# Attention and MLP on one core: first key halves on one queue, one load on GpSimd's queue, more late loads under way, and the last tiles stored by token

## The chip, the core and the metric

The kernel runs on one core of one Trainium2 chip. A core has a matrix engine (TensorE, PE in the profile), three engines for elementwise work (VectorE or DVE, ScalarE or ACT, GpSimd or POOL) and a queue engine (SyncE or SP), which here only starts transfers. ACT and POOL can start transfers too. The engines run side by side; each takes its own instructions strictly in the order in which the program issues them, and they wait for each other through semaphores. The metric is the device time of one launch in microseconds (us), the median of several runs.

## The reference

Linear attention with a product feature map, and behind it an MLP over all tokens. Sizes: batch B = 4, heads H = 4, sequence S = 1088, head dimension D = 32, r = 8; the MLP has width 128 and 2048 hidden units.

```python
def phi(x):                                   # 8 x 8 products per token
    a = np.einsum('rd,bhsd->bhsr', S1, x)
    b = np.einsum('rd,bhsd->bhsr', S2, x)
    return np.einsum('bhsi,bhsj->bhsij', a, b).reshape(*x.shape[:-1], r * r)
q_p, k_p = phi(q), phi(k)
kv = np.einsum('bhsf,bhsd->bhfd', k_p, v)
z = np.sum(k_p, axis=2)
num = np.einsum('bhsf,bhfd->bhsd', q_p, kv)
den = np.einsum('bhsf,bhf->bhs', q_p, z)[..., None] + 1e-06
x = (num / den).transpose(0, 2, 1, 3).reshape(B * S, H * D)
h = x @ w_in
g = np.maximum(h, 0.0) + alpha * np.minimum(h, 0.0)
out = g @ w_out
```

## The kernel before

The kernel builds a list of about 770 steps, and a table written out by hand, ORDER (L24 to L70), puts them into one sequence: each word names a step, the engine that runs it (p TensorE, a ACT, d DVE, g POOL, s SP) and the buffer slots that it takes. `arrange` (L98) reads the table, and the loop at L641 issues the steps in that sequence. So the order on every engine and queue is what ORDER says. A number behind p is a count of dummy work: before this step TensorE multiplies ones, so many blocks of 128 columns, in matmuls of up to 512 (`dummy`, L288).

*Attention.* Each batch has a key part (`keys`, L443) and a query part (`queries`, L509). Keys: two loads `ld_k…`, a transpose on DVE (`k…T`, L430), a feature matmul (`k…f`, L464), a transpose back (`k…fT`, L468), the 8 x 8 products on DVE or POOL (`k…p`, L484), the product with V (`kv…`, L504), a copy (`kvc`), a transpose on TensorE (`fin`) and a copy (`kvR`); beside it the sum over keys (`zs`, `z1`, `zS`, `C`). Queries: turn (`q…T`), feature matmul (`q…f`, L420), transpose (`q…fT`, L423), normaliser (`q…t`, `rc`, `b`), products (`q…p`), transposes (`q…PT`, L527), product with kvR (`q…n`, L534) and copies into the MLP's input (`q…x`, L542). Batch 0 is cut finer, so that work starts early: keys in two halves of 18 and 16 rows (`k0.0`, `k0.1`), queries in three pieces, c and d of 8 rows (loads `qa0`, `qa1`) and b of 18 rows (load `qb`). S1 and S2, one kilobyte each, are the two loads `rows` and `rows_1`; every feature matmul needs them, through `rowsT` (L312), `Wk` and `Wf`.

*MLP* (`mlp`, L571). Ten token tiles: 0 and 1 have 256 tokens, 2 to 8 have 512, 9 has the 256 tokens that are left over (64 of each batch). A tile has 16 steps `h` (x by one 128-column block of w_in, L590), 16 ReLUs `r` on ACT or DVE (L596, L598) and 16 steps `o` (ReLU by (1 − alpha) w_out, summed in one PSUM bank, L583; tile 9: L581), and one step `W` that adds x by w_in diag(alpha) w_out, a matrix built once (`winT`, `w_b`, `w_hi`, `w_lo`, `Wmm`, `W`). Twelve ReLU buffers and eight PSUM banks limit how far h runs ahead of o. Tiles 0 to 8 give the output transposed: a DVE transpose of 32 x 32 blocks (`oT`, L604) and four stores of 128-byte rows, 64 KB each for a 512-token tile (`store_main`, L616). Tile 9 has the tokens as the weights of its o matmuls, so that its sums come out by token, in two banks of 128 tokens; two copies (`oT9.0`, `oT9.1`) and two stores follow.

*Loads* (`load`, L196). All come through SP's queue but three on ACT's (k0.0, S1, alpha). A load of more than 64 KB waits on its queue until the third-last such load before it has landed (AHEAD = 3; six for k0, v0 and qa). V loads also wait for a POOL memset (`pads`, L232). Batch 3 reuses the key and query tiles of batch 0.

## Time and profile before

| | |
|---|---|
| runs | 108.78, 108.81, 109.87 us; median 108.81 |
| the profiled execution | 109.35 us; its span, first to last instruction, 107.6 us |
| PE busy | 97.0 us (90%) |
| PEld (weight loads) | 51.8 us |
| DVE / ACT / POOL busy | 82.8 / 65.4 / 47.2 us |
| read / written | 8.79 MB / 2.23 MB |
| the chain that ended last | PE 59%, DMA 28%, DVE 5%, SP's queue 3% of the span |

A profiled execution records every instruction with its start and its length. The page sums them by engine; the view of the chain follows the work that ended last back from step to step; the timeline lists instructions in order of time, merging neighbours of one kind (x3 is three of them); the stretches give the busy time of each engine between two times. An engine that is busy is not always useful (dummies, a slow clock), and an engine that idles costs nothing unless the end waits for it. The profile marks what ended an idle time with an arrow and the last releaser that it could see.

### The profile page before, as it was taken

The numbers are of one execution on the slowest core, as the hardware profiler recorded it, in microseconds if no ns is written. First come the engines' busy times: TensorE is split into PE (matmuls) and PEld (weight loads), VectorE is DVE, ScalarE is ACT, GpSimd is POOL, SyncE is SP. The second block draws the span as 40 slices with busy tenths as digits, with TensorE's granted clock in tenths as the row PEclk, the third lists the DMA queues.
The fourth block names the chain that finished last, engine by engine and source line by source line (L and its number), as shares of the span: only waits on it lengthen the run. The fifth ranks groups of instructions, "written<-read, shape, count | busy, mean of one in ns | idle before, by whom it ended". The sixth has DMA issues, their size and how long they took to land.

```text
span 107.6 us, 3569 instructions
## 1 busy us (share of the span) xinstructions
PE 97.0 (90%) x1476; PEld 51.8 (48%) x1489; DVE 82.8 (77%) x138; ACT 65.4 (61%) x150; POOL 47.2 (44%) x51
## 2 busy tenths in 40 slices
PE   7829979999989949999999999999999999999940
...
PEclk9995579999999999999999999999999999999998
...
GB/s 80 247 227 226 232 195 223 214 211 229 197 175 168 121 169 244 46 6 0 90 39 42 0 6 0 24 75 126 6 0 11 35 0 96 30 57 62 53 154 70
DMA packets 24769, 11.25 MB, mean 105 GB/s; under 512 B 17696, under 2 KB 22320, under 8 KB 24752
## 3 DMA queue, kind: packets, MB, share of 16 engines
...
HBM read 8.79 MB, written 2.23 MB: 102 GB/s over the span
## 4 chain that ended last, share of the span: by engine, by line
PE 59%; DMA 28%; DVE 5%; SPq 3%; issue 1%; DVEq 0%
PE ps L583 23%; PE ps L590 23%; DMA q<-in_q_dram 12%; DMA k<-in_k_dram 10%; PE ps L534 4%; SPq L200 3%; PE ps L504 3%; DMA v<-in_v_dram 3%; DMA w_in_f<-in_moe_w_in_dram 3%; PE ps L581 2%; PE ps L420 1%; DVE Q__71 L527 1%; DVE T__64 L430 1%; DVE T__65 L430 1%; PE ps L384 1%
## 5 line engine op out<-in xcount | busy, mean ns | idle before, releaser
L590 PE MATMUL ps<-x,w_in_bf 128*128 128x512 bf16 (+1 forms) x142 | 40.4, 356 | 0.4 <-issue 0.2
L590 PEld LDWEIGHTS <-w_in_bf 128*128 128x128 bf16 x160 | 15.0, 97 | 15.5 <-issue 3.1
L583 PEld LDWEIGHTS <-w_a_bf 128*128 128x128 bf16 x144 | 13.7, 98 | 12.8 <-issue 1.3
L192 POOL TENSOR_TENSOR P__69<-F__66 128x1152 f32<-128x1152 f32 (+1 forms) x8 | 15.5, 1948 | 8.0 <-DVE F__66 L192 7.7
L527 DVE STREAM_TRANSPOSE Q__71<-P__69 128x1152 f32<-128x1152 f32 (+2 forms) x9 | 10.4, 1167 | 0.1
L596 ACT ACTIVATE rh__87<-ps 128x512 bf16<-128x512 f32 (+1 forms) x11 | 5.9, 541 | 5.1 <-PE ps L590 5.0
L291 PE MATMUL ps<-const-bfloat16-1.0 128*128 128x512 bf16 (+3 forms) x24 | 7.9, 445 | 1.1 <-PEq L658 0.8
L192 POOL TENSOR_TENSOR P__70<-Fk__67 128x1280 f32<-128x1280 f32 (+1 forms) x4 | 8.6, 2161 | 0.0
L430 DVE STREAM_TRANSPOSE T__64<-k 128x1088 f32<-128x1088 f32 (+2 forms) x5 | 5.4, 1072 | 3.5 <-DMA k<-in_k_dram 3.5
L423 DVE STREAM_TRANSPOSE F__66<-ps 128x1152 f32<-128x1152 f32 (+2 forms) x6 | 5.9, 983 | 2.6 <-PE ps L420 2.0
L534 PE MATMUL ps<-Q__71,kvR 32*32 32x288 f32 (+2 forms) x384 | 7.7, 332 | 0.1
L596 ACT ACTIVATE rh__79<-ps 128x512 bf16<-128x512 f32 (+1 forms) x11 | 5.9, 540 | 1.8 <-PE ps L590 1.6
L596 ACT ACTIVATE rh__84<-ps 128x512 bf16<-128x512 f32 (+1 forms) x10 | 5.6, 558 | 1.0 <-PE ps L590 1.0
L598 DVE TENSOR_SCALAR rh__86<-ps 128x512 bf16<-128x512 f32 (+1 forms) x6 | 3.6, 594 | 3.1 <-PE ps L590 3.0
L185 ACT CAST x<-ps 128x576 bf16<-128x576 f32 (+2 forms) x6 | 3.1, 514 | 4.7 <-PE ps L534 4.6
L596 ACT ACTIVATE rh__85<-ps 128x512 bf16<-128x512 f32 (+1 forms) x8 | 4.3, 541 | 2.6 <-PE ps L590 1.7
L596 ACT ACTIVATE rh__83<-ps 128x512 bf16<-128x512 f32 (+1 forms) x9 | 4.7, 527 | 1.8 <-PE ps L583 1.0
L534 PEld LDWEIGHTS ps<-Q__71,kvR 32*32 32x32 f32 x384 | 4.5, 103 | 2.8 <-DVE F__66 L423 1.1
L596 ACT ACTIVATE rh__86<-ps 128x512 bf16<-128x512 f32 (+1 forms) x9 | 4.7, 526 | 1.2 <-PE ps L590 1.2
L192 POOL TENSOR_TENSOR P__69<-Fk__68 128x1024 f32<-128x1024 f32 (+1 forms) x2 | 4.3, 2166 | 1.7 <-DVE Q__71 L527 1.7
L583 PE MATMUL ps<-rh__86,w_a_bf 128*128 128x512 bf16 (+1 forms) x14 | 4.9, 349 | 0.1
L598 DVE TENSOR_SCALAR rh__81<-ps 128x512 bf16<-128x512 f32 (+1 forms) x7 | 4.1, 593 | 0.8 <-PE ps L590 0.8
...
## 6 DMA issues: line engine op xcount, KB each, us to landing
...
w_in_f<-in_moe_w_in_dram SPq DMA_DIRECT2D x4, 256.0 KB, 3.8
w_out_f<-in_moe_w_out_dram SPq DMA_DIRECT2D x4, 256.0 KB, 4.1
...
k<-in_k_dram ACTq DMA_DIRECT2D x1, 288.0 KB, 2.8
```

What stands on the lines that cost most here:

```text
L192: (nc.vector if e == "dve" else nc.gpsimd).tensor_tensor(out=dst, in0=a, in1=b, op=what)
L200: i = (nc.sync if e == "sp" else nc.scalar).dma_start(dst, src)
L291: nc.tensor.matmul(PS[:, 7, :128 * m], ones(128), ones(128 * m), start=True, stop=True, skip_group_check=True)
L423: return op({"dve": V(4 * n) + 60}, lambda e: nc.vector.transpose(bview(sb(F), [[n, 4], [1, n]]), ps(bf)[:, :, :n]), [o1], [bf, F], name=f ...
L430: os.append(op({"dve": V(n * 32) + 10}, lambda e, lo=lo, n=n: nc.vector.transpose(sb(bT)[:, lo * 32:(lo + n) * 32], src[:, lo:lo + n].rear ...
L504: nc.tensor.matmul(ps(bk)[32 * h:32 * h + 32, :R], v_sb[b][:, h, j], bview(sb(P), [[1, R]], (4 * j + h) * R), start=j == 0, stop=j == JG - ...
L527: ts.append(op({"dve": V(R * n1) + 20}, lambda e, lo=lo, n1=n1: nc.vector.transpose(bview(sb(Q), [[1, R * n1]], lo * R), bview(sb(P), [[1, ...
L534: nc.tensor.matmul(ps(bn)[32 * h:32 * h + 32, g, :n], kvR[b][32 * g:32 * g + 32, y, 32 * h:32 * h + 32], bview(sb(Q)[32 * g:32 * g + 32], ...
L583: nc.tensor.matmul(ps(bo)[:, :n], w, rhs, start=first, stop=end, skip_group_check=True)
L590: nc.tensor.matmul(ps(b)[:, lo:lo + m], w_in_bf[:, c], x(), start=True, stop=True, skip_group_check=len(parts) > 1)
L596: nc.scalar.activation(sb(br)[:, :n], ps(b)[:, :n], ACTF.Relu)
L598: nc.vector.tensor_scalar_max(sb(br)[:, :n], ps(b)[:, :n], 0.0)
```

## The change

1. Both halves of batch 0's keys load through ACT's queue, first and second there; before, the second half was second on SP's.
2. S1 loads through POOL's queue, behind `pads9` and ahead of `ident` (POOL's first step before); ACT's queue loses it. The copy `identb` moves from ACT to POOL.
3. On SP's queue qb stands ahead of V and of all weights, then come all four parts of w_in, then w_out1, w_out2, k1, w_out0, q1, w_out3, and v1 ahead of k3 and of batch 2's V. Loads of v2, v3, q3 may have six under way, k2, q2, k3 and v1 four.
4. ORDER is written anew throughout, with 103 dummy blocks in place of 91.
5. Tile 8 is computed like tile 9: each o step is four matmuls of 128 columns with the tokens as weights, summed in one bank; two copies of 256 columns on ACT take the place of the DVE transpose, and the four stores have rows of 512 bytes.
6. Tile 9's sums run half by half: the o step of each block is split into `o9.c` (first 128 tokens) and `o9.ch` (last 128), each half has its own copy; the first half goes out in one store, the second in two of 64 tokens.

```diff
 ORDER = """
-ld_rows_1:s ident:g ld_k0.0:a ld_rows:a rowsT:p26:0 selP:g zero:d M2:d ld_k0.1:s ld_w_in1:s ld_alpha:a k0T0:d:0 pads:g wz:g table:a Wk:d k0f0:p6:1
-k0T1:d k0f1:p ld_qa0:s M4:d ld_v0_3:s pads9:g identb:a qaT0:d ld_qa1:s k0fT0:d:0 zs00:p5:3 S2m:p:4 k0fT1:d ld_v0:s win1:a ld_v0_1:s qaT1:d S2q:d
-k0F1:a:1 k0p3:d:0 k0p4:d ld_v0_2:s k0p2:d zs01:p z10:a:0 zS0:p8 k0p0:g Wf:a C0:a k0p1:g alT:p:0 alTc:a qcf:p6:2 qcfT:d:0 qct:d:0 qcrc:d:0 qcb:d
-qcp0:d:1 kv00:p:6 kv01:p kv02:p kv03:p ld_w_in0:s win0:a qdf:p:1 qdfT:d:0 kv04:p ld_w_in2:s kvc0:a:0 qdt:g:0 ld_w_out0:s winT0:p:5 ld_qb:s w_b0:g
-qcPT0:d:0 ld_w_out1:s fin0:p3 kvR0:a qcn:p17:1 win2:a ld_k1_1:s winTc0:a qcx0:a oma:d qdrc:d:0 qdb:g qbT:d w_a1:a qdp0:d:0 qdPT0:d:0 qbf:p11:0 qbfT:d:0
...
-h9.7:p:1 r9.1:a:7 h9.14:p:6 r9.9:d:4 o9.4:p o9.15:p st5.3:s r9.8:d:10 st8.3:s o9.0:p st7.3:a o9.3:p r9.7:d:3 st7.0:a o9.8:p o9.9:p o9.2:p o9.7:p o9.1:p
-o9.5:p r9.14:d:2 o9.14:p oT9.1:d oT9.0:a st9.1:s st9.0:a
+ld_k0.0:a pads9:g ld_k0.1:a ld_rows:g ld_rows_1:s zero:d ident:g rowsT:p27:0 ld_qa0:s M2:d k0T0:d:0 ld_qb:s M4:d ld_alpha:a table:a pads:g Wk:d k0T1:d
+wz:g identb:g k0f0:p8:1 k0f1:p4 selP:g Wf:a ld_qa1:s qaT0:d ld_v0_1:s k0fT0:d:0 ld_v0_3:s zs00:p9:0 S2m:p:3 ld_v0:s k0fT1:d zs01:p k0F1:a:1 S2q:d
+ld_v0_2:s z10:a:0 zS0:p8 C0:a qcf:p8:2 k0p4:d:0 k0p2:d k0p3:d ld_w_in0:s win0:a k0p0:g kv00:p:0 ld_w_in1:s alT:p:6 k0p1:g kv01:p kv02:p kv03:p kv04:p
+kvc0:a:0 alTc:a ld_w_in2:s qcfT:d:0 qaT1:d qct:d:0 qcrc:d:0 qcb:d qcp0:d:0 win1:a qdf:p:1 qdfT:d:0 qcPT0:d:0 fin0:p14 kvR0:a qdt:g:0 qdrc:d:0
+ld_w_in3:s ld_w_out1:s qcn:p17:0 qbT:d oma:d qbf:p8:4 win2:a qdb:g qcx0:a win3:a h0.6:p:0 r0.6:a:0 qdp0:d:0 qdPT0:d:0 qbfT:d:0 w_b1:g h0.1:p:1 r0.1:d:1
+h0.14:p:2 r0.14:a:2 qbt:d:0 ld_w_out2:s w_a2:g ld_k1_1:s ld_k1:s ld_w_out0:s ld_q1:s h0.10:p:3 h0.7:p:0 r0.7:d:3 qbrc:d:0 qbb:g r0.10:a:4 h0.3:p:2
+r0.3:a:5 winT1:p:3 h0.11:p:2 qdn:p:4 qdx0:d w_a1:a o0.6:p:0 winTc1:a h0.9:p:1 h0.12:p:4 r0.12:a:0 h0.5:p:5 r0.11:d:6 qbp0:g:0 ld_w_out3:s h1.2:p:6
+r0.5:a:7 r0.9:a:8 h1.6:p:2 w_a0:g k1T0:d:0 winT0:p:3 ld_q1_1:s r1.6:a:9 h1.11:p:4 r1.11:a:10 r1.2:d:11 qbPT0:d:0 o0.11:p h0.4:p:5 h1.7:p:7 o0.10:p
+qbp1:g r1.7:a:4 h1.3:p:1 winTc0:a o1.6:p:2 w_b0:g o0.7:p r0.4:d:3 h1.14:p:4 k1f0:p:6 r1.3:a:9 o1.2:p o1.7:p k1fT0:d:0 o0.5:p h1.9:p:3 r1.9:d:7 o0.3:p
+h0.0:p:1 r0.0:d:5 k1p1:g:1 r1.14:a:4 qbPT1:d ld_k2_1:s o0.1:p h0.2:p:5 r0.2:a:1 h1.1:p:4 o0.9:p h1.5:p:6 r1.5:a:8 h1.12:p:7 r1.12:a:11 o0.4:p zs10:p:3
+r1.1:a:3 ld_k2:s ld_v1:s z11:d:0 h1.10:p:1 r1.10:d:6 o1.11:p ld_v1_3:s w_a3:a o1.5:p ld_v1_2:s o1.9:p o0.0:p q1T0:d:0 o0.2:p qbn:p:4 qbx0:d o1.10:p
+qbx1:a w_hi0:a k1p0:g o1.12:p o0.12:p ld_v1_1:s zS1:p C1:d h0.15:p:1 r0.15:a:0 o1.1:p h2.4:p:3 r2.4:a:3 ld_q2_1:s k2T0:d:1 q1f:p:4 q1fT:d:0 h2.6:p:1
+r2.6:a:11 o1.14:p h2.15:p:3 r2.15:a:4 o0.14:p o0.15:p w_hi1:a w_b2:g h2.1:p:1 r2.1:a:0 o1.3:p h2.13:p:3 h1.15:p:4 r1.15:d:9 r2.13:a:2 q1t:g:0 ld_k3:s
...
+r2.12:a:11 w_b3:g w_lo0:g r2.7:a:4 r2.9:a:1 kv10:p:6 h1.0:p:4 r1.0:a:5 h2.5:p:7 r2.8:d:7 ld_v2_3:s o2.1:p zs20:p:5 kvc1:a:0 h1.13:p:4 o2.4:p r2.5:a:0
+w_hi2:a q1b:d q1p0:d:0 o2.9:p h2.0:p:3 ld_v3_3:s r1.13:d:8 h2.3:p:7 z12:d:0 q1PT0:d:0 r2.0:a:1 h2.10:p:4 o2.12:p zS2:p o2.8:p fin1:p kvR1:d Wmm0:p:3
...
+h9.12:p:3 r9.12:d:11 r8.12:a:1 o8.5:p o8.15:p r9.9:a:8 o8.12:p W8:p r9.7:d:4 o8.7:p h9.8:p:0 h9.6:p:3 r9.8:a:5 W9:p h9.13:p:1 r9.13:a:1 h9.11:p:7
+o8.4:p o9.15:p o9.15h:p h9.4:p:0 h9.1:p:2 st7.1:s o9.10h:p r9.6:d:7 r9.4:d:0 o9.13:p o9.8:p o9.6:p st1.1:s o9.13h:p h9.0:p:1 r9.0:d:1 h9.14:p:3 W9h:p
+o9.6h:p h9.5:p:0 r9.5:d:7 o9.7:p o9.8h:p oT8.0:a:1 st8.1:s o9.2:p o9.9:p r9.1:a:3 o9.4:p r9.11:a:9 o9.11:p o9.11h:p r9.14:a:10 o9.0:p oT8.1:a o9.1:p
+o9.12:p o9.3:p o9.12h:p o9.0h:p o9.14:p st8.0:s o9.5:p oT9.0:a o9.4h:p o9.2h:p st8.3:s o9.5h:p o9.7h:p o9.14h:p o9.3h:p st8.2:s o9.1h:p st9.0:a o9.9h:p
+oT9.1:d st9.1:s st9.2:a
 """
...
@@ -194,10 +195,10 @@
     loads, issued = {}, []
 
     def load(name, eng, dst, src, nbytes, rate, deps=()):
-        ahead = 6 if name[:2] in ("k0", "v0", "qa") else AHEAD
+        ahead = 6 if name[:2] in ("k0", "v0", "qa", "v2", "v3", "q3") else 4 if name[:2] in ("k2", "q2", "k3", "v1") else AHEAD
 
         def emit(e):
-            i = (nc.sync if e == "sp" else nc.scalar).dma_start(dst, src)
+            i = {"sp": nc.sync, "act": nc.scalar, "pool": nc.gpsimd}[e].dma_start(dst, src)
             if nbytes > 65536:
                 if len(issued) >= ahead:
                     tc.add_manual_dep(i.ins, issued[-ahead].name, mybir.DependencyInfo(mybir.DependencyClass.Sync, mybir.DependencyReason.DATA))
@@ -253,10 +254,10 @@
                  dram(v, (b * H * S + JG * g) * D, [[NJ * D, 32], [S * D, H], [1, n * D]]), 32 * H * n * D * 4, 290., deps)
 
     for i, x in enumerate((S1, S2)):
-        load("rows", (("act", "sp")[i],), rows[i:2 * r:2], dram(x, 0, [[D, r], [1, D]]), 1024, 100.)
+        load("rows", (("pool", "sp")[i],), rows[i:2 * r:2], dram(x, 0, [[D, r], [1, D]]), 1024, 100.)
     load("alpha", ("act",), al, dram(moe_alpha, 0, [[128, NC], [1, 128]]), 8192, 200.)
     for i, (lo, n) in enumerate(((0, 18), (18, 16))):
-        load_rows(f"k0.{i}", k_sb[0][:, lo:lo + n], k, 0, lo, n, eng=("act", "sp")[i])
+        load_rows(f"k0.{i}", k_sb[0][:, lo:lo + n], k, 0, lo, n, eng="act")
     for i in range(2):
         load_rows(f"qa{i}", q_sb[0][:, 8 * i:8 * i + 8], q, 0, 8 * i, 8)
     load_v(0, [c_pads])
@@ -568,20 +569,22 @@
         src, os = turned(f"q{b}", q_sb[b], [got(f"q{b}")])
         xs[b] = queries(b, f"q{b}", src, os[0], JG)
 
-    def mlp(g, parts, store, final=False):
+    def mlp(g, parts, store, final=0):
         n = sum(m for m, _, _ in parts)
-        bo = Buf("ps", 2 if final else 1)
-        seq, done = [], [0]
-
-        def acc(rhs, w):
-            first, end = done[0] == 0, done[0] == NC
-            done[0] += 1
-            if final:
+        bo = Buf("ps", 2 if final == 2 else 1)
+        seq, done = [], [0, 0]
+
+        def acc(rhs, w, half=None):
+            first, end = done[half or 0] == 0, done[half or 0] == NC
+            done[half or 0] += 1
+            if final == 2:
+                nc.tensor.matmul(ps(bo)[:, half, :DM], rhs[:, 128 * half:128 * half + 128], w, start=first, stop=end, skip_group_check=True)
+            elif final:
                 for j in range(n // 128):
-                    nc.tensor.matmul(ps(bo)[:, j, :DM], rhs[:, 128 * j:128 * j + 128], w, start=first, stop=end, skip_group_check=True)
+                    nc.tensor.matmul(ps(bo)[:, 128 * j:128 * j + 128], rhs[:, 128 * j:128 * j + 128], w, start=first and j == 0, stop=end, skip_group_check=True)
             else:
                 nc.tensor.matmul(ps(bo)[:, :n], w, rhs, start=first, stop=end, skip_group_check=True)
-        cost = {"pe": 56 * n / 128 if final else n / 2.4 + 2.6}
+        cost = {"pe": 56 if final == 2 else 56 * n / 128 if final else n / 2.4 + 2.6}
         for c in range(NC):
             b, br = Buf("ps"), Buf("rh")
             need, lo = [], 0
@@ -597,8 +600,21 @@
                 else:
                     nc.vector.tensor_scalar_max(sb(br)[:, :n], ps(b)[:, :n], 0.0)
             seq.append((c, op(AD(n), re, need, [b, br], name=f"r{g}.{c}"), br))
-        last = [op(cost, lambda e, c=c, br=br: acc(sb(br)[:, :n], w_a_bf[:, c]), [o, c_wa[c // 4]], [bo, br], name=f"o{g}.{c}") for c, o, br in seq]
-        last.append(op(cost, lambda e: acc(whole[g](), W_bf), [c_W] + [d for _, _, ds in parts for d in ds], [bo], name=f"W{g}"))
+        halves = []
+        for half in range(2) if final == 2 else (None,):
+            at = bo if half is None else (bo, half, half + 1)
+            last = [op(cost, lambda e, c=c, br=br, half=half: acc(sb(br)[:, :n], w_a_bf[:, c], half), [o, c_wa[c // 4]], [at, br],
+                       name=f"o{g}.{c}" + ("", "h")[half or 0]) for c, o, br in seq]
+            last.append(op(cost, lambda e, half=half: acc(whole[g](), W_bf, half), [c_W] + [d for _, _, ds in parts for d in ds], [at],
+                           name=f"W{g}" + ("", "h")[half or 0]))
+            halves.append(last)
+        if final == 1:
+            boT = Buf("oT")
+            for j in range(2):
+                to = lambda j=j: bview(sb(boT), [[1, 256]], 256 * j)
+                o = op(AD(256), lambda e, j=j, to=to: copy(e, to(), ps(bo)[:, 256 * j:256 * j + 256]), last, [bo, boT], name=f"oT{g}.{j}")
+                store(g, o, boT, to, j)
+            return
         if not final:
             boT = Buf("oT")
             o = op({"dve": V(n) + 60}, lambda e: nc.vector.transpose(sb(boT).rearrange("p j f -> p (j f)")[:, :n], ps(bo)[:, :n]), last,
@@ -607,11 +623,11 @@
             return
         for j in range(2):
             t = consts.tile([128, DM], F32, tag=f"of{j}", name=f"of{j}")
-            o = op(AD(128), lambda e, j=j, t=t: copy(e, t, ps(bo)[:, j, :DM]), last, [(bo, j, j + 1)], name=f"oT{g}.{j}")
+            o = op(AD(128), lambda e, j=j, t=t: copy(e, t, ps(bo)[:, j, :DM]), halves[j], [(bo, j, j + 1)], name=f"oT{g}.{j}")
             store(g, o, t, j)
 
-    def put_out(g, i, o, boT, dst, src):
-        op({"sp": 450, "act": 450}, lambda e: (nc.scalar if e == "act" else nc.sync).dma_start(dst, src()), [o], [boT], name=f"st{g}.{i}", nbytes=65536, rate=150.)
+    def put_out(g, i, o, boT, dst, src, rate=200.):
+        op({"sp": 450, "act": 450}, lambda e: (nc.scalar if e == "act" else nc.sync).dma_start(dst, src()), [o], [boT], name=f"st{g}.{i}", nbytes=65536, rate=rate)
 
     def store_main(b, lo, n):
         def st(g, o, boT):
@@ -620,11 +636,21 @@
                                               ap=[[NJ * DM, 32], [DM, n // 32], [1, 32]]), lambda i=i: sb(boT)[32 * i:32 * i + 32, :n // 32])
         return st
 
+    def store_token_major(b, lo):
+        def st(g, o, boT, src, j):
+            for y in range(2):
+                dst = bass.AP(tensor=out.tensor, offset=(b * S + lo // 32 + 8 * j + 4 * y) * DM, ap=[[DM, 4], [NJ * DM, 32], [1, DM]])
+                put_out(g, 2 * j + y, o, boT, dst, lambda y=y: src()[:, 128 * y:128 * y + 128], 300.)
+        return st
+
     def store_last(g, o, t, j):
-        def f(e):
-            (nc.scalar if e == "act" else nc.sync).dma_start(
-                bass.AP(tensor=out.tensor, offset=(32 + j) * DM, ap=[[NJ * DM, 32], [S * DM, B], [1, DM]]), t)
-        op({"act": 600, "sp": 600}, f, [o], name=f"st{g}.{j}", nbytes=65536, rate=250.)
+        for y in range(1 + j):
+            n = 128 // (1 + j)
+
+            def f(e, y=y, n=n):
+                (nc.scalar if e == "act" else nc.sync).dma_start(
+                    bass.AP(tensor=out.tensor, offset=(32 + j + n // B * y * NJ) * DM, ap=[[NJ * DM, n // B], [S * DM, B], [1, DM]]), t[n * y:n * y + n])
+            op({"act": 600, "sp": 600}, f, [o], name=f"st{g}.{j + y}", nbytes=512 * n, rate=250.)
 
     def cols(b, lo, n):
         return lambda: x_sb[:, b, lo:lo + n]
@@ -635,8 +661,11 @@
     last = len(tiles_)
     whole[last] = lambda: xr.rearrange("p y s b -> p (y s b)")
     for g, (b, lo, n, needs) in enumerate(tiles_):
-        mlp(g, [(n, whole[g], needs)], store_main(b, lo, n))
-    mlp(last, [(256, whole[last], xrs)], store_last, True)
+        if g == last - 1:
+            mlp(g, [(n, whole[g], needs)], store_token_major(b, lo), 1)
+        else:
+            mlp(g, [(n, whole[g], needs)], store_main(b, lo, n))
+    mlp(last, [(256, whole[last], xrs)], store_last, 2)
 
     for o in arrange(ops, classes):
         early[0] &= o.name[:2] != "zs"
```

64 lines of the change are left out of this document (26 added, 38 removed).

## The prediction

> **What bounds the kernel now.** I read three views: the 40 slices for the shape, the chain of work that ended last in order of time, and then the stretches and the timeline where these two disagree with "TensorE is busy".
>
> ```profile
> PE   7829979999989949999999999999999999999940
> PEclk9995579999999999999999999999999999999998
> 2.00:4.00 2.00, 1.71 (x5) 0.44 (x3) 0.44 (x1) 1.16 (x1) 1.34 (x7) 1.00 0.74 190
> 4.00:6.00 2.00, 1.17 (x26) 0.50 (x26) 0.53 (x2) 0.51 (x3) 0.00 (x0) 1.00 0.96 317
> 6.00:8.00 2.00, 0.76 (x17) 0.33 (x18) 1.75 (x5) 0.62 (x1) 0.00 (x0) 0.93 0.71 211
> 8.00:10.00 2.00, 1.98 (x22) 1.12 (x22) 1.57 (x5) 0.61 (x3) 1.95 (x2) 0.50 0.75 198
> 10.00:12.00 2.00, 2.00 (x47) 0.82 (x47) 0.93 (x3) 0.85 (x3) 0.14 (x1) 0.50 0.74 249
> 12.00:14.00 2.00, 2.00 (x93) 1.83 (x96) 1.46 (x6) 0.00 (x0) 0.00 (x0) 0.50 0.76 237
> 38.00:40.00 2.00, 0.50 (x23) 0.35 (x26) 1.62 (x3) 1.99 (x7) 2.00 (x2) 1.00 0.56 142
> ```
>
> Columns of the stretches: length, busy time of PE, weight loads, DVE, ACT, POOL, then granted clock, DMA share, GB/s. From 20 us to 100 us TensorE is full with two exceptions, so what is not TensorE's own work is ahead of 20 us, at 38 to 40 us (1.5 of 2 us idle) and behind the last matmul. From about 8 to 14 us it is busy at half the clock. The 40 slices hide that: they print 9 there.
>
> ```profile
> 4.19 0.27 PE L312 MATMUL ps<-ident,rows 16*32 16x16 f32 x8 [0.48 <-DMA rows<-in_S_dram]
> 4.82 0.53 PE L464 MATMUL ps<-T__64,Wk 64*32 64x144 f32 x16
> 6.01 0.71 DVE L430 STREAM_TRANSPOSE T__64<-k 128x512 f32<-128x512 f32 x1 [1.29 <-DMA k<-in_k_dram]
> 6.87 0.53 PE L464 MATMUL ps<-T__64,Wk 64*32 64x144 f32 x16 [1.51 <-DVE T__64 L430]
> 9.33 1.61 DVE L192 TENSOR_TENSOR P__69<-ps,Fk__67 128x512 f32<-128x512 f32 x3
> 11.97 1.95 PE L504 MATMUL ps<-P__69,v 128*32 128x64 f32 x64
> 14.78 0.37 ACT L185 COPY kvs__76<-ps 128x256 f32<-128x256 f32 x1 [3.21 <-PE ps L504]
> 15.35 0.62 PE L374 MATMUL ps<-identb,w_in_bf 128*128 128x128 bf16 x8 [0.64 <-ACT kvs__76 L185]
> 17.21 0.85 PE L534 MATMUL ps<-Q__71,kvR 32*32 32x64 f32 x64
> 18.15 0.37 ACT L185 CAST x<-ps 128x256 bf16<-128x256 f32 x1
> 19.19 0.50 PE L590 MATMUL ps<-x,w_in_bf 128*128 128x256 bf16 x3
> 22.44 0.71 PE L464 MATMUL ps<-T__64,Wk 64*32 64x288 f32 x16
> ```
>
> Columns: start, length, engine, line, operands, in brackets the idle time before and its releaser. This is the way to the first MLP matmul at 19.19: S1 and S2 land (4.19), the second half of the keys lands (6.0), TensorE has stood still 1.5 us by then, runs at half clock soon after, and reaches kv0 only at 11.97, though its products were ready at 10.94 and its last V quarter, by the queue below, at 9.5. kv0 (its copy waits 3.21 us for it, to 14.78), the query product (17.21) and its copy (18.15) follow one another.
>
> ```profile
> 1.18 1.24 ACTq L200 DMA_DIRECT2D rows<-in_S_dram  x1
> 9.52 0.39 SPq L200 DMA_DIRECT2D w_out_f<-in_moe_w_out_dram  x1
> 18.55 2.22 SPq L200 DMA_DIRECT2D q<-in_q_dram  x2
> 21.07 0.38 SPq L200 DMA_DIRECT2D w_out_f<-in_moe_w_out_dram  x1
> 25.18 0.33 SPq L200 DMA_DIRECT2D v<-in_v_dram  x1
> 27.31 0.33 SPq L200 DMA_DIRECT2D k<-in_k_dram  x1
> 39.61 0.35 SPq L200 DMA_DIRECT2D q<-in_q_dram  x1
> 34.62 1.24 DVE T__64 L430
> 39.68 1.21 PE ps L504 x72
> k<-in_k_dram ACTq DMA_DIRECT2D x1, 288.0 KB, 2.8
> k<-in_k_dram SPq DMA_DIRECT2D x1, 256.0 KB, 4.4
> q<-in_q_dram SPq DMA_DIRECT2D x1, 288.0 KB, 4.8
> ```
>
> An issue on the SP queue waits until the third-last large load before it has landed (L202), so issues date landings: at 9.52 the last V quarter of batch 0 was in, at 21.07 w_in3, at 25.18 w_out3, at 27.31 the second half of k2, at 39.61 the V quarter that kv1 lacked. The last three rows give KB and us from issue to landing. kv1 starts at 39.68: the idle stretch at 38 to 40 us ends on that load as much as on the VectorE step named for it. Adding sizes in issue order, 3.79 MB were in by about 20.4 (second issue of the pair at 18.55), 4.06 MB by 21.07, 4.87 MB by 25.18.
>
> The sum is made against the profiled execution: 109.35 us, span 107.6. It is 0.5 us above the median of 108.81, which the result is taken from.
>
> **The change part by part.** *Head.* k0.1 moves from SP's second place (4.4 us to landing at 6.0) to ACT's second place (1.18, where S1 is now), beside only S2 and qa0 until k0.0 is in; qb must wait for k0.0. Bounds for its landing: 6.0 as now, and 4.0, if it took k0.0's 2.8 us from there. I take 4.85, since 688 KB (both halves and qa0) have to pass, and the stretches moved 0.42 MB by 4.0 (21 and 190 GB/s) and then 317 GB/s. ACT loses the S1 issue (1.24 us) and gains k0.1's; alpha and the table load come no later. The copy identb goes from ACT to POOL, and S1 with it: POOL now issues S1 ahead of ident, M2 and the memsets that SP's V loads wait for. No row shows a POOL DMA. Nearest: the same kilobyte on ACT, 1.24 us to issue and 3.0 us from issue to use; farthest, the slowest load of the three, 4.8 us. Issued at about 1.0, that is use at 4.0 or 5.8. I take 4.2, as now, the nearest row; 5.8 costs 1.1 us of the walk below.
>
> The walk: first turn done at 4.35 and Wk at 4.8; second turn 4.85 to 5.55; second feature product 5.6 to 6.1, ahead of it 4 dummy blocks where the 1.5 us idle was. Dummies are 103 blocks of 128 columns in place of 91, and stand in each of the waits from there to fin0. I take full clock from here. Then transposes to 6.9, S2q at 7.7, products 1.61 us to 9.35, last V quarter 9.6 (1.67 MB instead of 1.64 MB ahead of its end), kv0 9.6 to 10.8 (72 matmuls, 1.21 as at 39.68), copy to 11.4 behind win0, fin0 12.2, kvR0 12.65, 17 dummies, product 13.2 to 14.05, copy to 14.45, qbf, first h at 15.1. Against 19.19 that is −4.1: 1.1 from the earlier keys, 3.0 from the clock. Half of the busy time at half clock (8 to 14, 5.98) gives the same 3.0.
>
> *What the loads take back.* w_in0 to w_in3 now all come ahead of any w_out, and qb ahead of V. k1 ends at 3.80 MB, w_out0 at 4.06, q1 at 4.88: by the landings above 20.4, 21.1 and 25.2, no earlier than their like now. TensorE's written order puts 22 MLP matmuls of 256 columns (2.4 us), winT0, winT1 (0.62 each), qdn (0.85, as at 17.21) and k1f0 (0.71) between first h and o1.2, 5.2 us from 15.1; but k1f0 waits for k1's turn (1.24, as at 34.62) to about 21.8 and ends at 22.5. The order of before has k1f0 ending at 23.15 with 15 MLP matmuls (1.64 us), one winT and qdn done. So it is 0.65 earlier with 1.4 us more done: of the 4.1 us, 2.0 is left there, +2.1. From there to q1f (q1 in at 25.2, plus the turn) TensorE has 4.6 us of written work for 4.0 us, so the 2.0 holds.
>
> *More late loads.* k2, q2, k3, v1 may have four under way, v2, v3, q3 six. By themselves they hide behind TensorE's work; but v1 is moved ahead of q2, k3 and v2 and ends at 6.0 MB, some 31 us, while kv1 comes in the written order at about 31.5. So kv1's idle 1.5 us goes: −1.5. What is late next: DVE has k2's turn ahead of q1fT, k2 lands at about 27.3, as q1f ends; POOL's k1 and q1 products; ACT, which gets nearly all ReLUs there. New stalls between 0 and 1.5 (the one that goes); I take 0.4, nearer to the lower, because the slices show no other of that size from 20 to 100 us.
>
> *Tile 8.* Its 17 output steps become 68 of 128 columns with the tokens as weights.
>
> ```profile
> 93.89 1.29 PE ps L583 x6
> 102.24 1.24 PE ps L581 x22
> 103.50 0.29 DVE of L187
> 103.74 0.67 ACTq L625 DMA_DIRECT2D out_dram<-of  x1
> 104.34 0.60 SPq L625 DMA_DIRECT2D out_dram<-of  x1
> out_dram<-oT__90 ACTq DMA_DIRECT2D x1, 32.0 KB, 1.5
> SPq L669 <- DMA out_dram<-of: 1.5, 1, 1.5
> ```
>
> 68 at 1.24/22 is 3.83 us, 17 at 1.29/6 is 3.66: +0.17. The transpose (DVE, 0.7) becomes two copies on ACT, which has room there. Four stores of 64 KB stay four issues, of 512-byte rows instead of 128-byte.
>
> *End.* The last sums run half by half: the same 34 matmuls, but the first half ends 8 matmuls (0.45 us) before the second, and its copy and store with it. Now: last matmul 103.47, copy to 103.79, SP's last issue at 104.34 behind another store, wait 1.5, end. After: the second half goes out in two stores of 32 KB (1.5 us to landing now) from both queues. ACT's is behind st9.0's issue (0.67), SP's behind st8.2, whose copy stands late in ACT's order. Best: SP free, −1.0; worst: four store issues in line, +0.2. I take −0.4.
>
> Sum: −4.1 + 2.1 − 1.5 + 0.4 + 0.17 − 0.4 = −3.3. 108.8 − 3.3 = 105.5 us.
>
> By the Trainium skill, "DMA: Bandwidth & Descriptors", Specifications, the first byte on the GpSimd path comes after about 1 us, on the sync and scalar path after about 0.6; an estimate by that page puts S1 0.4 us later, and the sum stays at −3.3, since the loads take 2.1 back anyway. No run here shows it.
>
> **The rivals.** *Half clock stays.* The 4.0 to 8.0 stretches show 1.9 us of TensorE work in 4, with no idle longer than 1.5, and the clock fell. The new order fills them with dummies, but much of what is left is 32-column work, and kv0 ran at half clock while busy. Then the head is 1.1 earlier instead of 4.1, nothing is taken back: −1.1 − 1.5 + 0.4 + 0.17 − 0.4 = −2.4, 106.4 us. The Trainium skill, "TensorE: Matmul & The Clock Gate", Part 1, says the clock falls after an idle window of about 3.4 us and that gaps below that are harmless. The trace does not agree: 1.51 us idle was enough, at 0.50 from 8.00. By that rule the idle that this change removes is not the cause and this rival would be the forecast, at 106.4 us.
>
> *The loads take nearly all.* If the weights set the pace to 25 us (ACT's win1 stands ahead of kvR0, win2 ahead of qcx0, each waiting for its load; w_a3 for w_out3) and k2's turn stops DVE, 3.6 is taken back and 1.5 of stalls come again: −4.1 + 3.6 − 1.5 + 1.5 + 0.17 − 0.4 = −0.7, 108.1 us. For it: the MB by time are no better than now. Against: 12 ReLU buffers let h run ahead of o.
>
> *S1 is late; slower.* Place: rowsT, behind it on TensorE everything. If POOL's DMA needs longer than any load shown, TensorE idles from the end of its 27 dummies (3.7), and with the idle comes the half clock (3.0). The terms behind the head give −1.5 + 0.4 + 0.17 − 0.4 = −1.3 with no lead, so it decides once delay plus 3.0 exceeds 5.4, that is S1 in use after 6.6. At 8.0: 3.8 + 3.0 − 4.1 = +2.7, sum +1.4, 110.2 us. For it: no row of a POOL DMA, and ident, M2 and the first turn stand behind its issue. Against: 1 KB.
>
> **How the numbers follow.** One per cent, 1.1 us, is about what a measurement of this kernel can tell from no change; faster is below 107.7. Forecast 0.55 (own range 103.4 to 107.0), half clock 0.17, loads take all 0.17, late S1 0.11. Faster: 0.53 + 0.14 + 0.04 = 0.71; same 0.17; slower 0.12. The range: low is no new stalls (−0.4), the best end (−0.6) and 1.1 less taken back, 103.4; high is 108.6, past the second rival; outside lie late S1 and small ends of the others.
>
> **What would show it.** Granted clock 1.0 from 4 us on; keys' second turn before 5.5; first h near 15; then TensorE gaps before k1f0, up to 22.5; kv1 with no wait near 32; q1n near 40 instead of 44.5; last matmul near 100.2; from it to the end 3.7 instead of 4.1. It would be wrong with S1 in use after 6.6, with k0.1 no earlier on ACT, or with DVE idle for k2 and k3 at 25 to 35.

## The result, and the profile after

The changed kernel takes 114.63 us (median of 4; 114.35 to 115.06), the kernel before 108.8 us beside it: a ratio of 1.0526, 95% interval 1.044 to 1.0612. The forecast was 105.5. The profiled execution took 114.72 us, its span is 112.6 (107.6 before). Medians below are over all executions; the ratios leave out the executions that ran slow throughout, so that the two can differ a little.

Rows picked from the timeline of the changed kernel: TensorE and VectorE up to the first MLP matmul, then TensorE at the end.

```profile
4.56 0.30 PE L313 MATMUL ps<-ident,rows 16*32 16x16 f32 x8 [0.74 <-DMA rows<-in_S_dram]
4.80 1.03 PE L292 MATMUL ps<-const-bfloat16-1.0 128*128 128x512 bf16 x2
5.20 0.71 DVE L431 STREAM_TRANSPOSE T__64<-k 128x512 f32<-128x512 f32 x1
9.63 0.61 PE L292 MATMUL ps<-const-bfloat16-1.0 128*128 128x512 bf16 x2
9.70 1.61 DVE L193 TENSOR_TENSOR P__69<-ps,Fk__67 128x256 f32<-128x256 f32 x3
11.83 0.99 PE L505 MATMUL ps<-P__69,v 128*32 128x64 f32 x56
12.75 0.39 PE L421 MATMUL ps<-qTa,Wf 32*32 32x64 f32 x30
15.49 0.27 PE L421 MATMUL ps<-qTa,Wf 32*32 32x64 f32 x2 [2.35 <-issue]
15.69 1.58 PE L292 MATMUL ps<-const-bfloat16-1.0 128*128 128x512 bf16 x4
17.49 1.95 PE L292 MATMUL ps<-const-bfloat16-1.0 128*128 128x512 bf16 x5
19.37 0.85 PE L535 MATMUL ps<-Q__71,kvR 32*32 32x64 f32 x64
21.18 1.30 PE L593 MATMUL ps<-x,w_in_bf 128*128 128x256 bf16 x6
...
105.86 0.22 PE L581 MATMUL ps<-w_a_bf,rh__85 128*128 128x128 bf16 x1
```

S1 is in use at 4.56 and the keys' second turn is done at 5.91. But two dummy matmuls of 512 columns take 1.03 us at 4.80 and 0.61 at 9.63: TensorE runs at about half speed at 4.80, although the stretches below print a clock of 1.00. kv0 ends at 12.82 (14.71 before), so the head is then 1.9 us ahead. Then TensorE stands still for 2.35 us in the middle of qdf, after 30 of its 32 matmuls, with "issue" as releaser: the profile shows nothing that it waited for. Behind the stop the dummies ahead of fin0 and qcn take 1.58 and 1.95 us, at half clock, and the first h comes at 21.18 instead of 19.19.

The stretches of the same execution (length, busy PE, weight loads, DVE, ACT, POOL; then granted clock, DMA share, GB/s):

```profile
0.00:13.20 13.20, 11.59 (x220) 4.88 (x221) 6.73 (x19) 3.29 (x9) 5.74 (x21) 1.00 0.66 189
13.20:15.40 2.20, 0.00 (x0) 0.00 (x0) 0.69 (x1) 0.65 (x3) 0.00 (x0) 1.00 0.72 207
16.00:18.00 2.00, 2.00 (x8) 1.11 (x7) 1.97 (x7) 0.27 (x1) 1.06 (x3) 0.50 0.96 242
38.00:40.00 2.00, 2.00 (x80) 1.30 (x69) 1.81 (x4) 1.73 (x5) 1.45 (x1) 1.00 0.60 143
```

The clock is at 0.50 from 16 us. The wait of kv1 at 38 to 40 us is gone, as forecast. The stores on SP's queue at the end, and its waits:

```profile
101.49 0.51 SPq L630 DMA_DIRECT2D out_dram<-oT__92  x1
102.06 0.48 SPq L630 DMA_DIRECT2D out_dram<-oT__89  x1
102.58 2.14 SPq L630 DMA_DIRECT2D out_dram<-oT__92  x1
104.76 0.49 SPq L630 DMA_DIRECT2D out_dram<-oT__89  x1
105.29 0.51 SPq L630 DMA_DIRECT2D out_dram<-oT__91  x1
106.33 2.50 SPq L630 DMA_DIRECT2D out_dram<-oT__90  x4
108.92 0.58 SPq L651 DMA_DIRECT2D out_dram<-of  x1
...
SPq L698 <- DMA out_dram<-of: 1.9, 1, 1.9
```

The last matmul ends at 106.08, and SP then has four stores of tile 8 and the last one still to issue. From there to the end it is 6.5 us, 4.13 before. The 5.0 us of span are 2.0 at the first h, 0.6 from there to the last matmul, 2.4 behind it.

### The profile page after: what moved, and what is told of

It reads as the page before. It is cut to its first block, busy times and chain, and to the rows that moved or that the text cites. A ratio compares the mean times of both kernels' runs of the same rounds, so it can differ in the third digit from the quotient of the medians.

```text
span 112.6 us, 3673 instructions
## 1 busy us (share of the span) xinstructions
PE 101.1 (90%) x1541; PEld 53.7 (48%) x1541; DVE 82.9 (74%) x141; ACT 66.1 (59%) x146; POOL 46.9 (42%) x51
## 3 DMA queue, kind: packets, MB, share of 16 engines
q10 hardware_dynamic: 4256, 1.12, 4.5%
## 4 chain that ended last, share of the span: by engine, by line
PE 82%; issue 5%; DMA 3%; ACT 2%; DVE 2%; POOL 0%; DVEq 0%; POOLq 0%; ACTq 0%
PE ps L593 28%; PE ps L586 22%; PE ps L292 7%; PE ps L535 5%; PE ps L505 4%; PE ps L584 3%; PE ps L421 3%; PE ps L465 3%; DMA rows<-in_S_dram 3%; PE ps L581 2%; PE ps L496 1%; DVE T__65 L431 1%; PE ps L375 1%; PE ps L398 1%; PE ps L408 1%
## 5 line engine op out<-in xcount | busy, mean ns | idle before, releaser
L593 PE MATMUL ps<-x,w_in_bf 128*128 128x512 bf16 (+1 forms) x144 | 41.0, 356 | 0.5 <-DVE x L188 0.2
L586 PEld LDWEIGHTS <-w_a_bf 128*128 128x128 bf16 x128 | 12.2, 98 | 11.6 <-issue 2.0
L193 POOL TENSOR_TENSOR P__69<-F__66 128x1152 f32<-128x1152 f32 (+1 forms) x7 | 14.5, 2079 | 1.0 <-DVE F__66 L193 0.8
L528 DVE STREAM_TRANSPOSE Q__71<-P__69 128x1152 f32<-128x1152 f32 (+2 forms) x10 | 11.3, 1126 | 1.4 <-PE ps L535 1.2
L292 PE MATMUL ps<-const-bfloat16-1.0 128*128 128x512 bf16 (+3 forms) x28 | 11.2, 534 | 0.8 <-PEq L687 0.8
L193 POOL TENSOR_TENSOR F__66<-F__66,rd__74 128x288 f32<-128x288 f32 (+2 forms) x4 | 2.1, 532 | 18.8 <-DVE rd__74 L520 12.1
L193 POOL TENSOR_TENSOR P__69<-Fk__67 128x512 f32<-128x512 f32 (+2 forms) x4 | 6.8, 1722 | 3.6 <-DVE Fk__67 L469 3.6
L599 ACT ACTIVATE rh__80<-ps 128x512 bf16<-128x512 f32 (+1 forms) x13 | 7.1, 547 | 1.2 <-PE ps L593 1.1
L599 ACT ACTIVATE rh__78<-ps 128x512 bf16<-128x512 f32 (+1 forms) x11 | 6.1, 559 | 2.2 <-PE ps L593 2.1
L599 ACT ACTIVATE rh__79<-ps 128x512 bf16<-128x512 f32 (+1 forms) x8 | 4.4, 544 | 5.0 <-PE ps L593 5.0
L599 ACT ACTIVATE rh__86<-ps 128x512 bf16<-128x512 f32 (+1 forms) x12 | 6.6, 551 | 1.1 <-PE ps L593 0.6
L599 ACT ACTIVATE rh__84<-ps 128x512 bf16<-128x512 f32 (+1 forms) x10 | 5.8, 575 | 2.0 <-PE ps L593 1.9
L599 ACT ACTIVATE rh__82<-ps 128x512 bf16<-128x512 f32 (+1 forms) x9 | 4.7, 525 | 2.9 <-PE ps L593 2.7
L188 DVE CAST x<-ps 128x576 bf16<-128x576 f32 (+2 forms) x6 | 3.7, 648 | 2.6 <-PE ps L535 2.6
L599 ACT ACTIVATE rh__81<-ps 128x512 bf16<-128x512 f32 (+1 forms) x9 | 4.7, 528 | 0.9 <-PE ps L593 0.9
L292 PEld LDWEIGHTS <-const-bfloat16-1.0 128*128 128x128 bf16 x28 | 2.9, 125 | 4.9 <-issue 4.6
L599 ACT ACTIVATE rh__88<-ps 128x512 bf16<-128x512 f32 (+1 forms) x7 | 3.9, 564 | 2.1 <-PE ps L593 2.1
```

What stands on the lines that cost most here:

```text
L188: nc.vector.tensor_copy(dst, src)
L193: (nc.vector if e == "dve" else nc.gpsimd).tensor_tensor(out=dst, in0=a, in1=b, op=what)
L292: nc.tensor.matmul(PS[:, 7, :128 * m], ones(128), ones(128 * m), start=True, stop=True, skip_group_check=True)
L528: ts.append(op({"dve": V(R * n1) + 20}, lambda e, lo=lo, n1=n1: nc.vector.transpose(bview(sb(Q), [[1, R * n1]], lo * R), bview(sb(P), [[1, ...
L586: nc.tensor.matmul(ps(bo)[:, :n], w, rhs, start=first, stop=end, skip_group_check=True)
L593: nc.tensor.matmul(ps(b)[:, lo:lo + m], w_in_bf[:, c], x(), start=True, stop=True, skip_group_check=len(parts) > 1)
```

## The experiments

Every kernel was timed against the kernel before on the same chip. First h, last matmul and tail (last matmul to end) are read from the timelines.

| run | median us | ratio to before (95%) | first h | last matmul | tail |
|---|---|---|---|---|---|
| before | 108.8 | 1 | 19.19 | 103.47 | 4.13 |
| changed | 114.63 | 1.0526 (1.044 to 1.0612) | 21.18 | 106.08 | 6.52 |
| e1_fill_40 | 112.31 | 1.0309 (1.0243 to 1.0375) | 17.92 | 103.09 | 6.41 |
| e2_store_order | 112.27 | 1.0277 (1.0194 to 1.036) | 20.47 | 105.35 | 5.05 |
| e3_keys_alone | 108.61 | none given | 18.40 | 101.57 | 4.23 |
| e4_ahead_alone | 108.24 | 0.9996 (0.9954 to 1.0037) | 19.30 | 102.05 | 4.45 |
| e5_last_forms | 110.61 | 1.0195 (1.0151 to 1.024) | 18.98 | 103.22 | 5.58 |
| e6_warm_before | 109.34 | 1.0014 (0.9958 to 1.007) | 19.73 | 102.48 | 4.22 |
| e7_qdf_behind | 116.3 | 1.0521 (1.0429 to 1.0614) | 17.11 | 108.33 | 6.57 |
| e8_count | 114.6 | one execution | 20.34 | 106.22 | 6.18 |
| e9_fill_and_end | 111.03 | 1.0223 (1.0177 to 1.0268) | 19.15 | 104.15 | 4.65 |
| e10_tile8 | 110.26 | 1.0129 (1.0077 to 1.018) | 18.48 | 102.37 | 5.43 |
| e11_halves | 109.16 | 1.0002 (0.9966 to 1.0037) | 18.31 | 102.38 | 4.22 |
| e12_new_head | 111.42 | 1.0136 (1.0068 to 1.0204) | 19.60 | 104.62 | 4.18 |
| e13_head_mended | 112.72 | 1.0354 (1.0284 to 1.0424) | 18.12 | 107.01 | 4.49 |
| e14_three_undone | 110.97 | 1.0207 (1.0133 to 1.0281) | 19.58 | 105.62 | 4.48 |
| e15_keys_ahead | 108.18 | 0.9968 (0.9928 to 1.0007) | 19.61 | 102.33 | 4.37 |
| e16_covered | 111.16 | 1.0088 (1.0019 to 1.0156) | 20.89 | 103.97 | 5.33 |
| e17_wlo3 | 114.18 | 1.0552 (1.049 to 1.0614) | 18.72 | 106.99 | 4.81 |
| e18_no_dummies | 113.38 | 1.042 (1.0356 to 1.0485) | 20.99 | 106.63 | 6.67 |

In e7 and e12 the PSUM bank with the transposed alpha is written over before oma reads it, so w_a holds other numbers there; the instructions are the same. First h, last matmul and tail are one execution's each. The head of before, unchanged in e4, e5, e10 and e11, gives a first h from 18.31 to 19.30, so a difference of less than 1 us there shows nothing.

**The stop behind kv0.** The theory: TensorE had used up the instructions it held, and the next ones came too late. EARLY is the most blocks that one dummy matmul takes ahead of zs; with 1 the same columns take more instructions.

```diff
 e8_count, of the changed kernel
-EARLY = 4
+EARLY = 1
```

> The changed kernel with its first 39 dummy blocks (ahead of rowsT, k0f0 and k0f1) issued as 39 matmuls of 128 columns instead of 10 of up to 512: the same columns, 29 matmuls and 29 weight loads more, all before 8 us. Theory: TensorE stops when it has used up the instructions it holds, a fixed number, so the stop moves 29 matmuls forward: from behind the 30th of qdf's 32 to its first, give or take one, or to the end of kv0, and is about as long (1.5 to 2.5 us). Rival: qdf waits for something of its own (its bank, its data), and the stop stays at qdf's 30th or is gone. Time about 114.6 in the first case.

The timeline, and a stretch, of e8_count:

```profile
12.43 0.24 PE L421 MATMUL ps<-qTa,Wf 32*32 32x64 f32 x1
13.79 0.40 PE L421 MATMUL ps<-qTa,Wf 32*32 32x64 f32 x31 [1.12 <-issue]
...
0.00:13.60 13.60, 10.73 (x219) 7.52 (x221) 7.25 (x20) 3.31 (x9) 5.73 (x21) 1.00 0.63 185
0.00:19.80 19.80, 14.60 (x345) 9.75 (x348) 10.69 (x28) 5.71 (x14) 8.37 (x25) 1.00 0.68 202
```

The stop moved from behind qdf's 30th matmul to behind its first, 29 earlier, as many as were added. Counted up to the stop, matmuls and weight loads are 441 in the changed kernel (220 + 221) and 440 here (219 + 221). The stop is shorter than expected here (1.12 us), but a second one came at 18.0, of 1.93 us, after 693: 253 further on. It is a count, and nothing of qdf's. In e2, e7, e15, e17 and e18 a stop stands at the 440th or 441st too, in three different steps. The same in the kernel before, with its idle time ahead of k0f1 filled:

```diff
 e6_warm_before, of the kernel before
-k0T1:d k0f1:p ld_qa0:s
+k0T1:d k0f1:p16 ld_qa0:s
```

> The kernel before with 16 dummy blocks of 128 columns ahead of the second key product (k0f1), where TensorE stood still for 1.5 us; nothing else. The prediction took 3.0 us from keeping the clock full in the head. Theory now: what stands behind kv0 at full clock is the fetch of the next instructions (it came in at about 14.0 in the profile of before and work behind it at 15.35), so full clock ends at a wait of 1 to 2 us near 13 to 15 us and brings at most 1 us: 107.8 to 108.8. Rival, the prediction as it stood: first h at about 16.2 and 105.8 us.

The stretches and the timeline of e6_warm_before:

```profile
0.00:13.80 13.80, 10.04 (x219) 4.81 (x220) 8.56 (x22) 3.82 (x10) 5.14 (x21) 1.00 0.71 210
...
10.20 1.11 PE L504 MATMUL ps<-P__69,v 128*32 128x64 f32 x64
11.56 0.31 PE L504 MATMUL ps<-P__69,v 128*32 128x64 f32 x4
14.03 0.30 PE L504 MATMUL ps<-P__69,v 128*32 128x64 f32 x4 [2.16 <-issue]
19.73 0.50 PE L590 MATMUL ps<-x,w_in_bf 128*128 128x256 bf16 x3
```

The clock held, kv0 ran at 10.20 in 1.1 us instead of 1.95, and TensorE stopped at the 439th instruction for 2.16 us, in kv0 itself; behind the stop the granted clock was 0.59 from 14 to 16 us and 0.56 from 16 to 18. Nothing was gained (1.0014). This is the prediction's largest term, the full clock in the head, put into the kernel before by itself, and it is worth nothing there. The queue that brings instructions fits the theory. The DMA view of the changed kernel from 13.0 to 14.2 us:

```profile
q8 instruction: 1, 0.02, 4.8%
```

It lists no such packet before 13.0, and this is the first. In e6 the first lies between 11.5 and 12.6, in the kernel before between 12.0 and 14.1; there TensorE reaches its 439th instruction only at 14.45, having run at half clock, and waits for the copy of kv0's sums anyway. The Trainium skill, "Runtime: NRT & Kernel Launch", Instruction fetch mechanics, has instructions fetched in blocks of 16 KiB, 256 instructions, and calls the cost of a block boundary mostly hidden. The blocks agree (0.02 MB, 253 between two stops), the hiding does not: the stop was 2.35 us here. Why the block comes no earlier was not looked into.

Covering the stop, and taking the dummies behind it away:

```diff
 e1_fill_40, of the changed kernel
-qdf:p:1 qdfT:d:0
+qdf:p40:1 qdfT:d:0
 e18_no_dummies, of the changed kernel
-fin0:p14 kvR0:a
+fin0:p kvR0:a
...
-qcn:p17:0
+qcn:p:0
```

> The changed kernel with 40 dummy blocks of 128 columns (about 2.15 us at 0.053 us each) ahead of qdf; nothing else is moved. Theory: in the changed kernel TensorE stood still from 13.14 to 15.49 inside qdf because its next instructions had not been fetched, and the idle time put the clock to half until 19.24, which doubled fin0's and qcn's dummies. The dummies add instructions too, so the fetch should come up in the same place; if it is only the idle time that lowers the clock, the stall is covered by the 40 blocks or follows them, the clock stays full, the first h matmul comes at about 19.4 instead of 21.18, and the time is 113 us (114.6 less 1.7). Rival: the fetch counts instructions, so the stall stays at 2.3 us behind the dummies, the clock falls as before, and the time grows by up to 2 us (116.5).

> The changed kernel without the 31 dummy blocks ahead of fin0 and qcn, nothing else. In its profile they took 1.58 and 1.95 us at half clock between the end of the stop and the query product; at full clock the same blocks take 0.94 and 1.09. Theory: the stop of 1.8 to 2.4 us stays, the dummies no longer stand in the path, qcn starts when its operand is turned (16.9 to 17.2 instead of 19.37), the first h comes at 18.6 to 19.6 instead of 21.18, and the time is 112.6 to 113.4. Rival: without them TensorE idles, the clock stays at half for another 3.4 us or longer over the work behind, and the time is 114 us or more.

The timeline of e1_fill_40:

```profile
11.37 2.36 PE L292 MATMUL ps<-const-bfloat16-1.0 128*128 128x512 bf16 x10
13.65 0.51 PE L421 MATMUL ps<-qTa,Wf 32*32 32x64 f32 x32
14.10 0.94 PE L292 MATMUL ps<-const-bfloat16-1.0 128*128 128x512 bf16 x4
15.09 1.09 PE L292 MATMUL ps<-const-bfloat16-1.0 128*128 128x512 bf16 x5
```

2.36 us of useless work ahead of qdf made the kernel 2.3 us faster: no stop, and the dummies behind it back at 0.94 and 1.09. Part of this timeline is chance: the two dummies that took 1.03 us at 4.80 took 0.61 here, and kv0 ended 1.4 us earlier, all ahead of the edit. e9 and e14 have the 40 dummies and the slow start, and their first h comes at 19.15 and 19.58; without the 40 it comes at 20.34 (e8), 20.47 (e2) and 21.18. From an equal start the 40 dummies are thus worth 0.8 to 2.0 us there. e18, which keeps the stop and drops the dummies, came to 113.38, within what was expected, but its interval overlaps that of the changed kernel, and its profiled execution (115.43 us) has the first h at 20.99 and not at 18.6 to 19.6, with the granted clock at 0.50 from 18 to 22 us, as its rival expected. The split of the 2.3 us into stop and clock is not settled by it.

**The end.** The theory: three late stores of tiles 4 and 1 stand in SP's last stretch.

```diff
 e2_store_order, of the changed kernel
-W7:p oT5:d:1 st5.1:s
+W7:p oT5:d:1 st4.2:s st4.3:s st1.1:s st5.1:s
...
-o8.8:p st4.2:s h9.10:p:6
+o8.8:p h9.10:p:6
...
```

> The changed kernel with three late stores of tiles 4 and 1 (st4.2, st4.3, st1.1) moved ahead of st5.1 on SP, nothing else. Theory: in the changed kernel SP issues without a pause from 101.5 to 109.5 and the last store, st9.1, goes out 2.5 us behind its copy only because these three (0.5, 2.1 and 0.5 us of issue) stand among tile 7's, 8's and 9's. Then the last SP issue comes at about 106.5 instead of 108.9 and the time falls to 112.3 us (2.0 to 2.4 less). Rival: the four st8 issues with 512-byte rows (2.5 us) or the memory that takes the bytes set the end; then the last issue moves by less than 0.7 us and the time by the same, 114 us.

The median is 2.4 us less, as expected. SP's queue in e2_store_order:

```profile
103.40 2.50 SPq L630 DMA_DIRECT2D out_dram<-oT__90  x4
106.01 0.72 SPq L651 DMA_DIRECT2D out_dram<-of  x1
```

The last store goes out 2.9 us earlier, but 0.7 of that is a head that was faster by chance (first h at 20.47, last matmul at 105.35). The tail, where the three stores stood, is 1.5 us shorter, so that they cost between 1.5 and 2.4 us. Of this, 1.6 us may be no store's own: st4.3's issue took 2.14 us at 102.58, and one issue of about 2.1 us also came in e1 (99.07) and e7 (104.83), in e1 at another store. The tail is still 5.05 and not 4.13. What is left was looked for in the two new forms, in the kernel before: both, then each alone.

```diff
 e5_last_forms: tile 8 and tile 9; e10_tile8: the first; e11_halves: the second
-oT8:d:3
+oT8.0:a:3 oT8.1:a
...
-o9.13:p:3
+o9.13:p:3 o9.13h:p
...
```

> The kernel before with the two changed forms alone: tile 8 token-major with 512-byte store rows, tile 9's sums in halves with its second half stored in two parts; order of everything else as before. Theory: the forms cost what the prediction gave them (+0.17 and -0.4), and the long tail of the changed kernel (6.5 us from the last matmul to the end, 4.1 before) comes from where its order puts the stores: then 108.0 to 109.0 us and a tail of 3.7 to 4.3. Rival: the form costs, since a 512-byte-row store takes SP 0.63 us to issue where the other took 0.47 to 0.49: then the tail is above 4.8 and the time 109.5 or more.

> The kernel before with tile 8 token-major alone (68 output steps of 128 columns, two copies on ScalarE, four stores of 512-byte rows); tile 9 as before. The two forms together took 2.1 us (110.61). If the rows of tile 8 are what costs (0.64 us of SP issue each for three in line, where 0.47 stood, and later landings behind them), this alone gives 109.8 to 110.6; if the halves cost, it stays at 108.5 to 109.0.

> The kernel before with tile 9's sums in halves alone, the second half stored in two parts (three last stores instead of two); tile 8 as before. If the rows of tile 8 are what costs, this gives the prediction's -0.4 or nothing: 108.0 to 108.8. If the halves cost (the third store's 0.6 us on ScalarE's queue, and SP's last one issued 1.0 us late behind it), 109.5 to 110.6.

The theory of e5 fell: the forms alone cost 2.1 us. e10 and e11 give most of it to tile 8's form, 1.3%; the halves are level, and the intervals of e5 and e10 overlap. SP's queue in e11_halves, with tile 8's stores as before, and its last wait:

```profile
99.20 1.40 SPq L629 DMA_DIRECT2D out_dram<-oT__92  x3
103.28 0.64 SPq L650 DMA_DIRECT2D out_dram<-of  x1
...
SPq L694 <- DMA out_dram<-of: 1.6, 1, 1.6
```

The same in e10_tile8, and how long two stores of tile 7 took from issue to landing:

```profile
98.76 1.94 SPq L632 DMA_DIRECT2D out_dram<-oT__92  x3
103.72 0.58 SPq L653 DMA_DIRECT2D out_dram<-of  x1
...
SPq L700 <- DMA out_dram<-of: 2.0, 1, 2.0
SPq L700 <- DMA out_dram<-oT__89: 0.4, 1, 0.4
SPq L653 <- DMA out_dram<-oT__92: 0.3, 1, 0.3
...
out_dram<-oT__89 SPq DMA_DIRECT2D x2, 64.0 KB, 3.7
```

Three stores of 64 KB take 1.94 us to issue with 512-byte rows and 1.40 with 128-byte rows, 0.65 against 0.47 each, and the last store waits 0.3 for one of them. But issue is the smaller part. SP issues its last store 1.35 us behind the last matmul, 0.90 in e11; the other 0.8 us of the longer tail (5.43 against 4.22) come behind that issue. The stores of tile 7 beside them land after 3.7 us, after 2.7 in the kernel before. Why they land later is open. The Trainium skill, "DMA: Bandwidth & Descriptors", Specifications, has 512 bytes as the least transfer for full rate. No gain of that kind shows here.

**Parts alone.** The key loads, the late loads, and both together, in the kernel before:

```diff
 e3: ld_k0.1:s -> :a, ld_rows:a -> :g ahead of ident; e15: e3 and e4
 e4_ahead_alone
-        ahead = 6 if name[:2] in ("k0", "v0", "qa") else AHEAD
+        ahead = 6 if name[:2] in ("k0", "v0", "qa", "v2", "v3", "q3") else 4 if name[:2] in ("k2", "q2", "k3", "v1") else AHEAD
```

> The kernel before with the move of the key loads alone: k0.1 issued by ScalarE in second place, S1 by GpSimd ahead of ident. Theory: this part does what the prediction said it would (second turn done about 0.8 to 1.1 us earlier, S1 in use below 4.7), but the clock is at half from 7.7 on as before, so at most 1 us comes out: time 108.0 (107.6 to 108.8). Rival: GpSimd's issue or the shifted loads cost something behind the head; then 109 to 110 us with the second turn just as early.

> The kernel before with the new numbers of late loads under way alone (four for k2, q2, k3, v1, six for v2, v3, q3). Theory: the stall of kv1 at 38 to 39.7 goes in part, since v1's loads no longer wait for the third-last; from 0.5 to 1.5 us less, 107.3 to 108.3. Rival: more loads at a time slow each other, k2 or q1 comes later and the sum is nothing or a loss: 108.8 to 110 us.

> The kernel before with two parts of the change only: the key loads (k0.1 on ScalarE, S1 on GpSimd) and the new numbers of late loads under way. Each alone measured level with before (108.61 and 108.24, where before had 108.70). Theory: what each gains (first h at 18.4 instead of 19.19; no wait of kv1) adds up a little: 107.5 to 108.5. Rival: both come out of the same slack, the loads that TensorE waits for anyway, and nothing is left: 108.5 to 109.3.

e4 and e15 are level; e3 has no ratio, and its median of 108.61 stands beside 108.70 for the kernel before. In e4_ahead_alone the stretch of kv1's wait is full:

```profile
38.00:40.00 2.00, 2.00 (x78) 1.41 (x77) 1.95 (x4) 2.00 (x7) 2.00 (x2) 1.00 0.87 297
```

The wait is gone and the time is not less. The profiled execution of the kernel before was a bad one for this wait (1.5 us): with the same loads there TensorE idles from 36 to 40 us for 1.3 us in e5, 0.9 in e10, 0.6 in e11, 0.4 in e3 and 0.05 in e6. e15 is the nearest to a faster version that was found, and its interval holds 1. Its profiled execution has the stop too, 1.60 us up to winT0 at 15.78, at the 440th instruction, and its first h at 19.61: kv0's sums were copied by 14.62 (15.15 in the kernel before), and winT0 still started 0.4 us later than the 15.35 of before.

**Together.**

```diff
 e9_fill_and_end: e1, e2 and
-o9.15h:p h9.4:p:0 h9.1:p:2 st7.1:s o9.10h:p
+o9.15h:p h9.4:p:0 h9.1:p:2 st7.1:s oT8.0:a:1 oT8.1:a st8.1:s st8.0:s st8.3:s st8.2:s o9.10h:p
 e14_three_undone: e9, with tile 8 and 9 in the form of before (oT8:d:1)
 e17_wlo3: e9 and
-w_hi3:a w_lo3:d w_lo1:g
+w_hi3:a w_lo3:g w_lo1:g
```

> The changed kernel with the 40 dummy blocks ahead of qdf, with st4.2, st4.3 and st1.1 ahead of st5.1, and with tile 8's two copies directly behind the r ops that follow its last sum and its four stores in one row behind st7.1. Theory: the two losses are separate and add: 2.3 us came out of each alone, so 110.0 us, and up to 0.7 less by the earlier copies (109.3 to 110.2). Rival: what the head gains is lost again behind it, or the stores of tile 8 hold the queue whatever the order: 111 us or more.

> The changed kernel with the three things undone that the runs named: 40 dummy blocks ahead of qdf (2.3 us alone), the three late stores of tiles 4 and 1 ahead of st5.1 (2.3 us alone), and tile 8 transposed with 128-byte rows and tile 9 without halves, as before (1.4 us for tile 8's form on the kernel before). Theory: these are the whole loss of 5.8 us, and the time is 108.3 to 109.5, level with before. Rival: what is left of the change (key loads, load order, more late loads, the new order of the middle) costs too, and the time stays at 110 us or more.

> The changed kernel with the 40 dummy blocks, the three stores moved and tile 8's copies earlier (111.03 us), and w_lo3 on GpSimd again instead of VectorE, where it took 2.22 us ahead of k3's and q2's turns. Theory: the one wait of TensorE left in the middle (0.5 us for T at about 47) goes, and 0.3 to 0.7 us with it: 110.3 to 110.8. Rival: GpSimd's own work then holds q1n back and it is level or slower: 111 us or more.

e9 gained 3.6 us, not 4.6: the rival's 111 us. e14 is no better than e9, and 2% above before. The three costs are thus not the whole loss. In the table, from first h to last matmul the changed order takes 84.9 us, e9 85.0 and e14 86.0, where e4 and e6, in the old order without kv1's wait, take 82.75. TensorE is busy for 83.8 us of this in the changed kernel and 82.5 in e4, so that 1.3 us are work and 0.8 are waiting. Some of the 2 us has a name in the changed kernel's trace: T for k3 waits behind w_lo3 on VectorE (0.5), two winT instead of one lie behind the first h (0.6), tile 8 (0.17). The rest is not found. e17 was to take the first away and failed: on GpSimd w_lo3 stood ahead of w_lo1, and Wmm, which builds W, waited 2.8 us. The waits of TensorE in e17_wlo3:

```profile
PE ps L385 <- POOL w_hl L193: 2.8, 1, 2.8
PE ps L375 <- issue: 1.0, 1, 1.0
PE ps L421 <- issue: 0.6, 1, 0.6
```

It also shows the stop for instructions again, at the 441st and the 696th, with the 40 dummies in place: they cover it in one execution and not in another.

**A head without the stop.** qdf's 64 instructions behind qcn, in the changed kernel (e7) and in the kernel before (e12, then e13 with qbT and oma earlier); e16 covers the stop there with 40 dummies.

```diff
 e7, e12, e13
-kv04:p ... qdf:p:1 qdfT:d:0 ... fin0 kvR0:a qcn
+kv04:p ... fin0 kvR0:a qcn:p17:0 qdf:p:4 qdfT:d:0
```

> The changed kernel with qdf (64 instructions of TensorE) moved from behind kv0 to behind qcn, its VectorE steps and qbf, qbT, qdn moved after it; no dummies added. Theory: TensorE comes to its 440th instruction only inside qcn, about 1.5 us later, so the wait for the next ones is under 1 us there, the clock stays up, the first h comes near 17 to 18 instead of 21.18, and the time is 111.0 to 112.2. Rival: the loss is qdf's or the head's own, the first h moves by less than 1 us and the time stays above 113.5.

> The kernel before with the key loads moved (k0.1 on ScalarE, S1 on GpSimd), the new numbers of late loads under way, 12 more dummy blocks (k0f1, zs00) to hold the clock, and qdf moved behind qcn; the end as before. Theory: full clock pays only where TensorE does not run out of instructions, and with qdf's 64 moved it reaches the 440th after the copy of kv0's sums; then the first h comes at 15.5 to 17, loads take back about 2 us of that as the prediction had it, and the time is 106.5 to 108.0. Rival: instructions run out anyway (in winT0, fin0 or qcn) or the weights set the pace, and the time is within 0.7 us of before.

> The kernel of the run before it (keys, late loads, 12 dummy blocks, qdf behind qcn, end as before), with qbT and oma put back ahead of qdf's steps on VectorE, where they hold nobody up: in that run qbf waited 2.24 us for qbT. Theory: without that wait the first h comes at 16.8 to 17.5 (19.19 in the kernel before), loads take back about 1 to 2 us, and the time is 107.0 to 108.3. Rival: the loads take back all of it, and the time is within 0.5 us of before whatever the head gains.

> The kernel before with the key loads and the late loads as in the run beside it, and in the head 12 more dummy blocks (k0f1, zs00) to hold the clock, kv0's last quarter ahead of qdf, and 40 dummy blocks ahead of qdf to cover the time until the next instructions are there. Theory: the clock stays up, the wait for instructions is covered behind kv0 where the copy of its sums has to be waited for anyway, and the first h comes at 17.0 to 18.0: 107.0 to 108.2. Rival: the 2.1 us of dummies cost what the clock brings, the first h stays above 18.4 and the time at 108.5 or more.

Waits of TensorE in e7_qdf_behind, then in e12_new_head, then in e13_head_mended:

```profile
PE ps L421 <- DVE omaT L337: 1.6, 1, 1.6
PE ps L535 <- issue: 0.6, 1, 0.6
```

```profile
PE ps L420 <- DVE qTb L561: 2.2, 1, 2.2
```

```profile
PE ps L590 <- ACT rh__79 L596: 1.7, 1, 1.7
PE ps L590 <- DVE rh__80 L598: 1.1, 1, 1.1
PE ps L534 <- DVE omaT L336: 1.1, 1, 1.1
```

In e7 the stop lies inside qcn and is 0.6 us, and the first h comes at 17.11, both as expected; the time does not follow. qbf and the MLP behind it then wait for VectorE, which got qdf's steps later, and the granted clock is 0.50 from 20 to 28 us. e12 has no stop at all, and e13 trades its wait of 2.2 for three of 1.1 to 1.7, with the clock at 0.50 from 24 to 28. e16 has no stop either, but its clock did not stay up (0.50 from 8 to 12 us), and it was 0.9% slower. Whether the head's gain can be had with the whole order planned anew was not tried.

## Why the prediction was wrong

*Key loads, S1.* Right: GpSimd's issue took 0.70 us, S1 was in use at 4.56 (4.2 forecast, trouble from 6.6), the second turn was done at 5.91 (5.55). The rival of a late S1 did not come.

*The clock.* This step failed first: "I take full clock from here". Products ended at 11.31 instead of 9.35 and kv0 at 12.82 instead of 10.8, as dummies and key products ran at half speed until about 9. Filling idle time is not enough by itself: of nine profiled executions with this head, two (e1, e17) took 0.61 us for the dummies at about 4.8 us and had kv0 done at 11.4; the others took 1.03 or 1.04, like the changed kernel. What decides between the two is open. The rival of the half clock had this part.

*kv0 to the first h.* This step failed most: "copy to 11.4 ... first h at 15.1". It priced work by the duration of its matmuls and took for granted that TensorE had its instructions. A stop of 2.35 us came in, e6 and e8 show that it is a matter of count, and e1 that removing it, with the clock that fell behind it, gives 2.3 us back in the median. From 15.1 to 21.18 it is 6.1 us: 2.0 by kv0, 2.35 by the stop, 1.5 by dummies at half clock (3.53 where e1 has 2.03), 0.2 left. So the head's -4.1 was +2.0. The Trainium skill, "TensorE: Matmul & The Clock Gate", Part 1, has the clock fall after an idle window of about 3.4 us. The trace does not agree here either: a stop of 2.35 us was followed by 0.50 from 16 to 18 us, while after 1.60 (e15) and 1.12 (e8) the clock stayed at 1.00.

*What the loads take back*, +2.1, was never called on, as the head had gained nothing. e1's first h came 3.26 us before the changed kernel's and its last matmul 2.99 before, so the loads took back at most 0.3 at 17.92; no run has a first h near 15.1.

*More late loads.* The mechanism was right, kv1's wait went; the size was off. -1.5 was one execution's, the same wait was 0.05 to 1.3 us in five others, and e4 measures 0.9996.

*Tile 8*, +0.17, was the output steps alone. "Four stores of 64 KB stay four issues" took their issue time as unchanged, and it rose from 0.47 to 0.63 us (2.50 for four). The form measured +1.4 us in e10, of which the issue is the smaller part; later landings, which the sum had at nothing, are the larger.

*End*, -0.4: the halves are level (e11). The worst case, "four store issues in line, +0.2", counted the stores of tiles 8 and 9 only; between them the order has st4.2, st4.3 and st1.1, and SP issued without a rest from 101.5 on. e2 gives 1.5 us in the tail and 2.4 in the median for taking these three away.

*What the sum left out.* Nothing was charged for the middle of the new order, which takes some 2 us more than the old one without kv1's wait. That is measured, and only in part explained.
